# The first transform of a long convolution as 32-row by 64-column matrix blocks at four row positions of TensorE, two token tiles side by side

## The chip, the core and the metric

The kernel runs on one core of a Trainium2 chip. The core has TensorE (PE in the profile, with its weight loads as PEld), VectorE (DVE), ScalarE (ACT), GpSimd (POOL) and SyncE (SP). Each engine runs its own instructions in a fixed order and waits on semaphores for the others. Matrix results land in PSUM, from which ACT or DVE copy them to the on-chip memory. Transfers are issued by SP, POOL or ACT. The metric is the device time of one execution in microseconds; the kernel before takes 1782.84 us, the median of three runs (1781.9 to 1785.29).

## What is computed

There are 2048 tokens of 576 channels. A conditioning vector `c` gives six vectors of 576 numbers (shift, scale and gate for two halves). The first half is a layer norm, then a long convolution per channel by FFT with a kernel made from 128 complex poles per channel. The second half is a gated MLP that mixes over tokens.

```python
mod = (_silu(c) @ w_mod).reshape(c.shape[0], 6, 1, -1)
sa, ca, ga, sb, cb, gb = (mod[:, 0], mod[:, 1], mod[:, 2], mod[:, 3], mod[:, 4], mod[:, 5])
h = _layernorm(x, axis=-1) * (1 + ca) + sa
x = x + ga * _A_ref(h, A_re, A_im, B_re, B_im, C_re, C_im, log_dt, Dskip)   # y = irfft(rfft(h) * rfft(K))
h = _layernorm(x, axis=-1) * (1 + cb) + sb
x = x + gb * _B_ref(h, w_in, w_sp, b_sp, w_out)                             # gated MLP over tokens
```

Only the transform of `h` (with `ga` already multiplied in) is changed here.

## The kernel before

The work has two parts. The first, `ssm`, makes the convolution and takes roughly the first 420 us; the rest is the MLP, in which TensorE is busy nearly all the time. Inside `ssm` an FFT of 2048 tokens is taken as 32 by 64: a first transform over 32 tokens that lie apart, then a second over 64.

**The loop.** `for tick in range(NG + 4)` runs over 36 groups of poles. In each tick, for group numbers shifted by some ticks, `t_unit` (L428, phases), `s_unit` (L440, sine and cosine on ACT), `p_unit` (L445, products on DVE), `kg_unit` (L461, matmuls that make the convolution kernel) and `k1_unit` (L477, its own first transform) run; `e_unit` (L416, exponentials) runs every third tick. In ticks 0 to 7 the first transform of the tokens runs too, two tiles of 128 tokens in each tick. From tick 9 on its place is taken by the second transforms (`u_unit`, `z_unit`, `v_unit`, `y_unit`).

**One token tile** (`ln_unit`, L393). A tile is 128 rows: four groups of 32 tokens, so its transform matrix is four 32 by 32 blocks on the diagonal of a 128 by 128 matrix, once for the real and once for the imaginary part. DVE makes `n = (x - mean) * cga` (L397) and scales the matrix rows by the inverse deviation, `rt` (L399). TensorE then makes two outputs (real, imaginary) of 128 by 576, in two halves of 288 columns. Each half is a bf16 matmul that adds the transformed shift (L405: `cs`, 96 rows, times `gsp`) and a float32 matmul `rt` times `n` (L406), into one PSUM tile of the ring `ps`, which has two buffers. ACT copies each finished `ps` to `st1o` (L407), and POOL stores a whole tile, 128 by 2 by 576, to `u1_d` in DRAM (L408); `st1o` has two buffers too. From tick 9 on `u_load` (L521) reads `u1_d` back with all 2 by 16 by 4 blocks on the partitions, and `u_unit` multiplies by `fwd`, whose rows are in that order.

**The shift.** The constant part of `h`, `sga = sa * ga`, is the same for all tokens, so only the column sums of the transform matrix are needed. To keep float32 accuracy in bf16, `sga` is split into three bf16 parts and the sums too; the six useful products stand in six rows among the 96 of `cs` and `gsp`. `mod_unit(0)` makes `gsp` with four ACT copies and two DVE subtractions (L339 to L344), on partition ranges that start at 0, 32 and 64.

**Loads.** `r1_load(i)` (L361) brings the matrices of one pair of tiles, 256 KB in float32 and 96 KB in bf16; `ln_load(i)` (L357) brings four tiles of tokens, 1152 KB, into the buffer of the four tiles before the last four. Both are on SP.

**What sets the order.** The units are written tick by tick, but a scheduler of the language sorts the instructions of each engine by its own estimates, so that the order on an engine isn't the order of the code. Instructions issued through `mlp.tied` keep the program's order and appear with line 140 in the profile, which is the line of that helper.

Of the kernel before, what the change touches and what calls it, by code (L numbers as in the profile page):

```python
# [9 lines left out]
F32 = mybir.dt.float32  # L10
# [21 lines left out]
def consts():  # L32
# [8 lines left out]
    for j in range(4):  # L41
        s = slice(32 * j, 32 * j + 32)
        r1[0, s, s] = np.cos(ang)
        r1[1, s, s] = -np.sin(ang)
    r1t = np.zeros((128, 16, 2, 128))
    st4 = np.zeros((128, 16, 2, 64))
    for t in range(16):
        for g in range(4):
            th = ang + 2 * np.pi * b4[4 * t + g] * (k1 + 0.25) / 2048
            s = slice(32 * g, 32 * g + 32)  # L50
            r1t[s, t, 0, s] = np.cos(th)
            r1t[s, t, 1, s] = -np.sin(th)
            hh, g2 = divmod(g, 2)
            o = slice(32 * g2, 32 * g2 + 32)
            st4[64 * g2:64 * g2 + 32, t, hh, o] = np.cos(th).T / 2048
            st4[64 * g2 + 32:64 * g2 + 64, t, hh, o] = -np.sin(th).T / 2048

    import ml_dtypes
    part = r1t.sum(0)
    cs = np.zeros((96, 16, 2, 128))  # L60
    for i in range(3):
        rows = part.astype(ml_dtypes.bfloat16).astype(np.float64)
        cs[i] = rows
        if i < 2:
            cs[32 + i] = rows
        if i < 1:
            cs[64 + i] = rows
        part = part - rows

    def forward(th):  # L70
# [7 lines left out]
    for h, sg in ((0, 1.0), (1, -1.0)):  # L78
# [19 lines left out]
    f = np.float32  # L98
    small = np.concatenate([np.eye(128), r1[0], r1[1], forward(th), st3a, st3b, ones], axis=1)
    return {"c_small": small.astype(f), "c_st": st2.astype(f), "c_r1t": r1t.astype(f), "c_st4": st4.astype(f),  # L100
            "c_sel": sel.astype(ml_dtypes.bfloat16), "c_cs": cs.astype(ml_dtypes.bfloat16)}

# [50 lines left out]
def ssm(tc, I, x1_d, consts_s, dram, mod_d, mlp):  # L153
# [5 lines left out]
    with ExitStack() as ctx:  # L159
# [156 lines left out]
        sga = ep.tile([128, D], F32, name="sga", bufs=1)  # L316
        gsp = ep.tile([96, D], BF, name="gsp", bufs=1)

        def mod_unit(k):
# [15 lines left out]
            elif k == 1:  # L335
                V.scalar_tensor_tensor(v3(cga), src, 1.0, v3(gar), op0=ALU.add, op1=ALU.mult)
            elif k == 0:
                V.tensor_tensor(v3(sga), src, v3(gar), op=ALU.mult)
                A.activation(gsp, sga[:96], AF.Copy)  # L339
                V.tensor_tensor(sga[:96], sga[:96], gsp, op=ALU.subtract)  # L340
                A.activation(gsp[32:64], sga[32:64], AF.Copy)
                A.activation(gsp[64:], sga[64:96], AF.Copy)
                V.tensor_tensor(sga[64:96], sga[64:96], gsp[64:], op=ALU.subtract)
                A.activation(gsp[64:], sga[64:96], AF.Copy)  # L344
            else:
                mrow = ep.tile([128, D], F32, name="gar", bufs=1)
                if k == 4:
                    A.activation(v3(mrow), src, AF.Identity, bias=one)
                else:
                    A.activation(v3(mrow), src, AF.Copy)  # L350
                G.dma_start(mod_d[k - 3:k - 2], mrow[0:1])
# [16 lines left out]
        def ln_stats(i):  # L368
# [3 lines left out]
            if i < 2:  # L372
                junk = ep.tile([128, 2, D], F32, name="st1o")
                ss = ep.tile([128, 4], F32, name="ss")
# [17 lines left out]

        def ln_unit(b):  # L393
            i, j = divmod(b, 4)
            nm, r = lns[i]
            n = x4s[i][:, j]
            V.scalar_tensor_tensor(n, n, nm[:, j:j + 1], cga, op0=ALU.add, op1=ALU.mult)  # L397
            rt = ep.tile([128, 2, 128], F32, name="rt")
            V.tensor_scalar(rt, r1t[b // 2][0][:, b % 2], r[:, j:j + 1], None, op0=ALU.mult)  # L399
            o = ep.tile([128, 2, D], F32, name="st1o")  # L400
            for ri in range(2):
                pm = ps2()
                for h in range(2):
                    c = slice(HC * h, HC * h + HC)
                    T.matmul(pm[:, h, :HC], r1t[b // 2][1][:, b % 2, ri], gsp[:, c], start=True, stop=False)  # L405
                    T.matmul(pm[:, h, :HC], rt[:, ri], n[:, c], start=False, stop=True)  # L406
                A.activation(v3(o[:, ri]), pm[:, :, :HC], AF.Copy)  # L407
            G.dma_start(u1_d[:, b].rearrange("r p d -> p r d"), o)  # L408

# [109 lines left out]
        def u_load(c, i):  # L519
            st[c, i] = u1 = part("u1", 5)  # L520
            S.dma_start(by(u1, c), u1_d.rearrange("r b (g k) d -> (r b g) k d", k=32)[:, kr(c, i), chan(c)])  # L521

# [106 lines left out]
        r1_load(0)  # L629
        ln_load(1)  # L630
        S.dma_start(dsk, I["dsk"])
        r1_load(1)
# [17 lines left out]
        for tick in range(NG + 4):  # L650
# [53 lines left out]
            if j < 8:  # L704
                if j in (2, 4):
                    ln_stats(j // 2 + 1)
                for b in (2 * j, 2 * j + 1):
                    ln_unit(b)
                if j < 6:
# [1437 lines left out]
```

## Time and profile before

| | |
|---|---|
| median of the runs | 1782.84 us |
| the profiled execution, its own time | 1788.13 us |
| its span in the profile | 1786.3 us |
| TensorE busy over the span | 94% |
| first transform, first matmul to last store issued | 54.1 to 159.3 us |
| its matmuls | 64 in bf16 (L405), 64 in float32 (L406, two records each, 128 in all) |

The page of the profile gives busy times for the whole span. The first transform lies in one stretch of some 105 us, so the views that count here are those of that stretch: busy time of each engine in pieces of 10 us, groups of instructions, and waits. `PEclk` is the clock that TensorE was granted, 1.00 for full speed. Line numbers such as L406 are those of the kernel before. A float32 matmul leaves two records of a weight load and two of a matmul.

### The profile page before, as it was taken

How to read it: one execution, taken by the hardware profiler on the slowest of the kernel's cores; microseconds unless marked ns; L12 is line 12 of the kernel's file. 1: busy time of each engine (PE TensorE's matmuls, PEld its weight loads, DVE VectorE, ACT ScalarE, POOL GpSimd, SP SyncE). 2: the span in 40 equal slices, each digit the busy share in tenths (PEclk: the TensorE clock that was granted, in tenths of full speed). 3: DMA queues.
4: the chain of work that ended last, by engine and by line, in shares of the span. 5: the costliest groups of instructions: out<-in, count | busy, mean ns of one | idle time of the engine just before them, and what ended most of it. 6: DMA issues, size and time to landing. Idle time of an engine off the chain costs nothing.

```text
span 1786.3 us, 35743 instructions
## 1 busy us (share of the span) xinstructions
PE 1686.7 (94%) x14830; PEld 1255.3 (70%) x14830; DVE 1266.6 (71%) x2331; ACT 854.4 (48%) x1129; POOL 227.0 (13%) x364
## 2 busy tenths in 40 slices
PE   3599899998899999999989999999999999999999
PEld 1355555565455445777878888888888888888887
DVE  6785999966998998688889677688344468344432
ACT  4778999954477666445434444234222224122210
POOL 2111223332122211000000000000111100111100
PEclk9789999998999999999999999999999999999999
DMA  9465646679688779777665886773766573556531
GB/s 268 145 198 179 196 120 167 176 204 304 206 260 266 249 228 264 284 248 250 240 209 164 282 299 233 269 253 118 250 225 226 203 231 100 193 195 215 194 111 40
DMA packets 182193, 377.80 MB, mean 212 GB/s; under 512 B 37680, under 2 KB 101552, under 8 KB 181264
## 3 DMA queue, kind: packets, MB, share of 16 engines
q1 hardware_dynamic: 140000, 177.29, 33.1%
q0 software_dynamic: 36128, 171.57, 28.9%
q10 hardware_dynamic: 5904, 26.67, 3.7%
q8 instruction: 116, 1.90, 0.4%
q14 instruction: 45, 0.37, 0.1%
HBM read 264.73 MB, written 101.31 MB: 205 GB/s over the span
## 4 chain that ended last, share of the span: by engine, by line
PE 58%; DVE 10%; DMA 8%; issue 4%; ACT 1%; POOL 1%; SPq 0%; ACTq 0%; DVEq 0%; POOLq 0%
PE ps L140 54%; DMA zset<-set_d 2%; DMA wsst<-in_w_spT 1%; DVE zset L140 1%; DVE bsz L140 1%; DMA win_d<-wso 1%; DVE n L140 1%; DVE gt L140 1%; DVE rq L140 1%; PE pk L527 1%; ACT z L140 1%; PE pk L540 1%; DMA ue<-v_d 1%; DMA z_d<-z 1%; DVE wsp L140 1%
## 5 line engine op out<-in xcount | busy, mean ns | idle before, releaser
L140 PEld LDWEIGHTS <-zset 128*128 128x128 f16 x7182 | 702.8, 98 | 95.3 <-DVE zset L140 9.5
L140 PE MATMUL ps<-wsp,zset 128*128 128x256 f16 x6048 | 669.2, 273 | 9.1 <-DVE zset L140 7.5
L140 PE MATMUL pz<-wz,nt 128*128 128x512 f16 (+1 forms) x1120 | 222.5, 358 | 12.3 <-ACT nt L140 5.3
L140 ACT ACTIVATE z<-gt 128x1024 f16<-128x1024 f32 x56 | 59.0, 1054 | 285.4 <-DVE gt L140 285.4
L140 PEld LDWEIGHTS <-nt 128*128 128x128 f16 x1120 | 108.7, 98 | 119.9 <-ACT nt L140 6.9
L140 DVE SCALAR_TENSOR_TENSOR gt<-ps,sc,bsp 128x512 f32<-128x512 f32 x36 | 27.0, 750 | 206.0 <-PE ps L140 204.3
L140 PE MATMUL ps<-wout,z 128*128 128x288 f16 x1344 | 170.0, 286 | 0.0
L1855 POOL DMA_DIRECT2D zset<-set_d x96 | 50.9, 530 | 872.0 <-PE ps L140 626.1
L140 PEld LDWEIGHTS <-z 128*128 128x128 f16 x1344 | 131.5, 98 | 33.0
L140 DVE TENSOR_TENSOR raw<-raw 128x512 f32<-128x512 f32 (+2 forms) x228 | 119.1, 528 | 13.0 <-DMA raw<-z_d 8.7
L140 PE MATMUL ps<-n2o,zset 128*128 128x256 f16 x1134 | 128.2, 273 | 0.0
L140 DVE SCALAR_TENSOR_TENSOR gt<-ps,sc,gt 128x512 f32<-128x512 f32 (+1 forms) x180 | 122.2, 696 | 7.6
L140 ACT ACTIVATE zset<-raw 128x1792 f16<-128x1792 f32 x48 | 81.2, 1691 | 60.8 <-PE ps L140 27.0
L140 DVE TENSOR_TENSOR zset<-raw,zset 128x1792 f16<-128x1792 f32 x48 | 97.0, 2020 | 15.6 <-ACT zset L140 15.6
L140 DVE TENSOR_TENSOR z<-ps,z 128x512 f32<-128x512 f32 (+1 forms) x126 | 72.0, 599 | 36.8 <-ACT z L140 26.7
L140 ACT ACTIVATE wsp<-raw,sc 128x1792 f16<-128x1792 f32 x25 | 44.6, 1784 | 42.7 <-DVE raw L140 35.0
L140 ACT ACTIVATE z<-z,sc 128x1024 f32<-128x1024 f32 x21 | 24.1, 1148 | 75.6 <-DVE z L140 71.9
L435 DVE SCALAR_TENSOR_TENSOR ft<-ft,ps 128x1024 f32<-128x1024 f32 x36 | 43.8, 1217 | 18.0 <-ACT ft L434 18.0
L140 ACT ACTIVATE z<-z,nm,r 128x1152 f32<-128x1152 f32 x24 | 31.4, 1341 | 51.6 <-DVE nm L140 29.5
L140 ACT ACTIVATE z<-pz,sc 128x512 f32<-128x512 f32 (+1 forms) x96 | 51.6, 583 | 9.2 <-PE pz L140 4.6
L140 PE MATMUL ps<-n2q,wf 128*128 128x512 f16 x252 | 55.7, 379 | 0.0
L140 PE MATMUL ps<-wout,z1b 128*128 128x288 f16 x384 | 52.4, 286 | 0.0
(361 smaller groups left out, 2512.0 us busy)
## 6 DMA issues: line engine op xcount, KB each, us to landing
zset<-set_d POOLq DMA_DIRECT2D x96, 896.0 KB, 5.0
raw<-z_d SPq DMA_DIRECT2D x48, 512.0 KB, 5.6
set_d<-zset ACTq DMA_DIRECT2D x24, 896.0 KB, 6.1
z_d<-z POOLq DMA_DIRECT2D x32, 576.0 KB, 9.4
zset<-wa_d POOLq DMA_DIRECT2D x18, 896.0 KB, 4.9
raw<-in_w_spT SPq DMA_DIRECT2D x25, 512.0 KB, 4.5
set_d<-zset SPq DMA_DIRECT2D x12, 896.0 KB, 5.2
u_d<-st1o POOLq DMA_DIRECT2D x16, 576.0 KB, 3.8
```

The source lines that it names most:

```text
L140: return self.tc.keep_in_program_order(f(*a, **k))
L435: V.scalar_tensor_tensor(f, f, MAGIC, pa, op0=ALU.subtract, op1=ALU.subtract)
L527: T.matmul(pm, fwd, u1, start=True, stop=True)
L540: T.matmul(pm[:, w * j:w * j + w], cst[k // 8][:, k % 8], k1t[c][:, k, :w], start=True, stop=True)
L1855: self.nc.gpsimd.dma_start(o, self.set_d[f, j - 1] if j else self.wa_d[f])
```

## The change

The matrix blocks on the diagonal are no longer put into one 128 by 128 matrix with zeros elsewhere. Each 32-row group `g` of a tile is multiplied by its own 32 by 64 block (32 real and 32 imaginary outputs), with the group's rows as the row position in the array. Tile `t` of a pair writes output partitions `64 t` to `64 t + 63`, and group `g` writes its own bank: `pms[g // 2]`, half `g % 2`. A pair of tiles is done in two halves of 288 channels, each with 8 bf16 and 8 float32 matmuls, four copies of 128 by 576 in all (L415 of the new file) and two stores of 128 by 4 by 288.

The shift is now added for each row group, so `gsp` needs its six rows in every group of 32 partitions. The subtractions are made on all 128 partitions with a mask `msk`, a new small constant whose entries are 0 or -1 (from partition 3 on the first part is taken off, from 5 on the second). The constants `r1t` and `cs` shrink to 32 columns, 64 KB and 32 KB per pair; `cs` has 128 rows. `u1_d` becomes `[4, 16, 2, 32, D]`, and the rows of `fwd` are put in that order, so `u_load` reads as many pieces of the same size as before. `rt` has four buffers in place of two. `junk` in `ln_stats` takes the new shape of `st1o`, of the same size.

```diff
-    r1t = np.zeros((128, 16, 2, 128))
+    r1t = np.zeros((128, 16, 2, 32))
...
-            r1t[s, t, 0, s] = np.cos(th)
-            r1t[s, t, 1, s] = -np.sin(th)
+            r1t[s, t, 0] = np.cos(th)
+            r1t[s, t, 1] = -np.sin(th)
...
-    part = r1t.sum(0)
-    cs = np.zeros((96, 16, 2, 128))
+    part = np.stack([r1t[32 * g:32 * g + 32].sum(0) for g in range(4)])
+    cs = np.zeros((128, 16, 2, 32))
...
+        for r in ((0, 3, 5), (1, 4), (2,))[i]:
+            cs[r::32] = rows
         part = part - rows
+    msk = np.zeros((128, 2))
+    for g in range(0, 128, 32):
+        msk[g + 3:g + 6, 0] = -1.0
+        msk[g + 5, 1] = -1.0
...
-        u1_d = dram.tile([2, 16, 128, D], F32, name="u1_d")
+        u1_d = dram.tile([4, 16, 2, 32, D], F32, name="u1_d")
...
-                A.activation(gsp, sga[:96], AF.Copy)
-                V.tensor_tensor(sga[:96], sga[:96], gsp, op=ALU.subtract)
-                A.activation(gsp[32:64], sga[32:64], AF.Copy)
-                A.activation(gsp[64:], sga[64:96], AF.Copy)
-                V.tensor_tensor(sga[64:96], sga[64:96], gsp[64:], op=ALU.subtract)
-                A.activation(gsp[64:], sga[64:96], AF.Copy)
+                for i in range(2):
+                    A.activation(gsp, sga, AF.Copy)
+                    V.scalar_tensor_tensor(sga, gsp, msk[:, i:i + 1], sga, op0=ALU.mult, op1=ALU.add)
+                A.activation(gsp, sga, AF.Copy)
...
-            r1t[i] = ep.tile([128, 2, 2, 128], F32, name="r1t"), ep.tile([96, 2, 2, 128], BF, name="cs")
+            r1t[i] = ep.tile([128, 2, 2, 32], F32, name="r1t"), ep.tile([128, 2, 2, 32], BF, name="cs")
...
-        def ln_unit(b):
+        def ln_rows(b):
...
-            rt = ep.tile([128, 2, 128], F32, name="rt")
-            V.tensor_scalar(rt, r1t[b // 2][0][:, b % 2], r[:, j:j + 1], None, op0=ALU.mult)
-            o = ep.tile([128, 2, D], F32, name="st1o")
-            for ri in range(2):
-                pm = ps2()
-                for h in range(2):
-                    c = slice(HC * h, HC * h + HC)
-                    T.matmul(pm[:, h, :HC], r1t[b // 2][1][:, b % 2, ri], gsp[:, c], start=True, stop=False)
-                    T.matmul(pm[:, h, :HC], rt[:, ri], n[:, c], start=False, stop=True)
-                A.activation(v3(o[:, ri]), pm[:, :, :HC], AF.Copy)
-            G.dma_start(u1_d[:, b].rearrange("r p d -> p r d"), o)
+            rt = ep.tile([128, 64], F32, name="rt", bufs=4)
+            V.tensor_scalar(rt, r1t[b // 2][0][:, b % 2].rearrange("p r k -> p (r k)"), r[:, j:j + 1], None, op0=ALU.mult)
+            return n, rt, r1t[b // 2][1][:, b % 2].rearrange("p r k -> p (r k)")
+
+        def ln_pair(b):
+            pair = [ln_rows(b), ln_rows(b + 1)]
+            for h in range(2):
+                c = slice(HC * h, HC * h + HC)
+                o = ep.tile([128, 4, HC], F32, name="st1o")
+                pms = [ps2(), ps2()]
+                for t, (n, rt, cs) in enumerate(pair):
+                    for x, y, st in ((cs, gsp, True), (rt, n, False)):
+                        for g in range(4):
+                            rows = slice(32 * g, 32 * g + 32)
+                            T.matmul(pms[g // 2][64 * t:64 * t + 64, g % 2, :HC], x[rows], y[rows, c], start=st, stop=not st, skip_group_check=True)
+                for k, pm in enumerate(pms):
+                    A.activation(o[:, 2 * k:2 * k + 2], pm[:, :, :HC], AF.Copy)
+                G.dma_start(u1_d[:, b:b + 2, :, :, c].rearrange("g b r k d -> (b r k) g d"), o)
...
+        S.dma_start(msk, I["c_msk"])
```

Besides what the code says, the scheduler puts some instructions in another order, in ticks 0 to 9 and hardly behind them. Three places follow. The numbers behind a name tell one buffer from another; new line numbers are up to 8 higher than the old ones.

On PE, the start of the first pair of tiles in tick 0 before (`ps` is the PSUM ring, `gsp` and `cs` the shift, `ln_x` the tokens `n`, `rt` the scaled matrix):

```order
L405 LDWEIGHTS cs_144
L405 MATMUL ps_462<-gsp_105,cs_144 128x288
L406 MATMUL ps_462<-ln_x_119,rt_459 128x288
...
L405 MATMUL ps_468<-gsp_105,cs_144 128x288
L406 MATMUL ps_468<-ln_x_119,rt_459 128x288
...
L405 MATMUL ps_479<-gsp_105,cs_144 128x288
L406 MATMUL ps_479<-ln_x_119,rt_476 128x288
```

The same place in the changed kernel:

```order
L413 LDWEIGHTS cs_145
L413 MATMUL ps_466<-gsp_105,cs_145 64x288
...
L413 MATMUL ps_466<-ln_x_120,rt_460 64x288 x2
...
L413 MATMUL ps_466<-ln_x_120,rt_463 64x288 x2
...
L413 MATMUL ps_467<-ln_x_120,rt_460 64x288 x2
...
L413 MATMUL ps_467<-ln_x_120,rt_463 64x288 x2
```

Before, one `ps` takes two bf16 and two float32 matmuls of one tile. Now one `ps` takes two row groups of the first tile (two bf16, then two float32, the row that ends in x2) and the same two row groups of the second tile; the other two row groups go to the next `ps`.

On DVE in tick 2, around the statistics of the third block of tokens (`bs`, `mv`), before:

```order
L276 TENSOR_TENSOR t_ph_359<-t_ph_359,t_rnd_301 128x432
L387 BN_STATS bs_606<-ln_x_572 128x6 x3
L388 BN_AGGR mv_607<-bs_606 128x2
L387 BN_STATS bs_606<-ln_x_572 128x6 x2
...
L454 TENSOR_TENSOR pg_674<-et_405,ft_502 128x512
```

and now:

```order
L278 TENSOR_TENSOR t_ph_360<-t_ph_360,t_rnd_303 128x432
L462 TENSOR_TENSOR pg_723<-et_406,ft_519 128x512
L463 TENSOR_TENSOR pg_723<-et_406,ft_519 128x1024
L210 TENSOR_TENSOR t_sq0_629<-t_ph_360,pt_628 128x432
L388 BN_STATS bs_639<-ln_x_605 128x6 x3
```

The statistics stood ahead of the products `pg` of `p_unit` and now stand behind two of them.

On ACT ahead of tick 0, between two exponentials `et`, before:

```order
L341 ACTIVATE gsp_105<-sga_104 32x576
L342 ACTIVATE gsp_105<-sga_104 32x576
L376 ACTIVATE st1o_370,nm_368<-ln_x_147 128x576
L426 ACTIVATE et_405<-pk_410 128x512
L344 ACTIVATE gsp_105<-sga_104 32x576
```

and now:

```order
L343 ACTIVATE gsp_105<-sga_104 128x576
L377 ACTIVATE st1o_371,nm_369<-ln_x_148 128x576
L431 ACTIVATE et_406<-ps_407 128x1024
L345 ACTIVATE gsp_105<-sga_104 128x576
...
L434 ACTIVATE et_406<-pk_411 128x512
L431 ACTIVATE et_414<-ps_415 128x1024
```

One of the four copies to `gsp` is gone, and one of the four sums over a token tile (`nm`) moved ahead of the third exponential, where it stood behind it.

More of the change, by code (lines that the diff above doesn't have):

```diff
@@ L98, in consts @@
     f = np.float32
[L99 removed]
+    fwd = forward(th).reshape(2, 16, 4, 128).transpose(2, 1, 0, 3).reshape(128, 128)
+    small = np.concatenate([np.eye(128), r1[0], r1[1], fwd, st3a, st3b, ones], axis=1)
     return {"c_small": small.astype(f), "c_st": st2.astype(f), "c_r1t": r1t.astype(f), "c_st4": st4.astype(f),
[L101 removed]
+            "c_sel": sel.astype(ml_dtypes.bfloat16), "c_cs": cs.astype(ml_dtypes.bfloat16), "c_msk": msk.astype(f)}
 def bc(ap, shape):
@@ L316, in ssm @@
         sga = ep.tile([128, D], F32, name="sga", bufs=1)
-        gsp = ep.tile([96, D], BF, name="gsp", bufs=1)
+        gsp = ep.tile([128, D], BF, name="gsp", bufs=1)
+        msk = cp.tile([128, 2], F32, name="msk")
         def mod_unit(k):
@@ L372, in ln_stats @@
             if i < 2:
-                junk = ep.tile([128, 2, D], F32, name="st1o")
+                junk = ep.tile([128, 4, HC], F32, name="st1o").rearrange("p (a b) d -> p a (b d)", a=2)
                 ss = ep.tile([128, 4], F32, name="ss")
```

10 lines of the change are left out of this document (2 added, 8 removed).

## The prediction

> **What bounds the kernel now.** I read the busy times in pieces of 10 us over the first transform, then the groups of instructions there with what ended their waits, then single stretches of the timeline. The sum is made against the profiled execution:
>
> ```profile
> span 1786.3 us, 35743 instructions
> ```
>
> Its own time is 1788.13 us, 1.8 beyond its span and 5.3 above the median of 1782.84; I work out a difference and take it from the median.
>
> ```profile
> core 0: us, PE busy (x) PEld busy (x) DVE busy (x) ACT busy (x) POOL busy (x), PEclk, DMA share, GB/s
> 50.00:60.00 10.00, 3.85 (x10) 2.20 (x10) 8.69 (x13) 9.87 (x18) 0.00 (x0) 0.50 0.01 4
> 60.00:70.00 10.00, 5.53 (x18) 2.96 (x17) 8.20 (x25) 9.94 (x17) 0.73 (x1) 0.84 0.19 69
> 70.00:80.00 10.00, 8.98 (x35) 5.10 (x35) 9.64 (x20) 7.13 (x12) 6.00 (x8) 0.66 0.53 159
> 80.00:90.00 10.00, 5.46 (x72) 3.14 (x71) 5.01 (x12) 4.59 (x5) 0.73 (x1) 0.85 0.79 266
> 90.00:100.00 10.00, 7.84 (x52) 3.87 (x50) 8.93 (x28) 9.47 (x13) 3.74 (x5) 0.67 0.48 162
> ...
> 120.00:130.00 10.00, 8.09 (x90) 4.89 (x88) 9.35 (x30) 4.75 (x8) 1.88 (x3) 1.00 1.00 334
> ...
> 105.00:160.00 55.00, 50.93 (x539) 31.05 (x535) 37.78 (x80) 42.22 (x58) 8.88 (x13) 1.00 0.59 192
> 200.00:250.00 50.00, 48.45 (x674) 27.83 (x674) 46.05 (x71) 47.92 (x63) 14.49 (x24) 1.00 0.38 111
> ```
>
> Three regimes show. Up to 100 us PE is not the bound: ACT is nearly full in three of the five pieces, PE works at a granted clock of 0.50 to 0.85, and 80 to 90 us is a stall in which transfers run and no engine is full. From 105 to 160 PE has the clock whole and is busy 50.93 of 55 us, ACT 42.22. Behind, in the loop, PE (48.45 of 50) and ACT (47.92) are both nearly full, so I take it that time won or lost before 160 us reaches the end undiminished.
>
> Who waits for the first transform between 48 and 162 us, and then ACT between 105 and 160:
>
> ```profile
> L406 PE MATMUL ps<-ln_x,rt 128*128 128x288 f32 x128 | 47.3, 465 | 0.0
> L407 ACT ACTIVATE st1o<-ps 128x576 f32<-128x576 f32 x32 | 20.4, 647 | 14.9 <-DMA u_d<-st1o 8.1 <-PE ps L406 5.8 <-ACT et L426 0.3
> L408 POOL DMA_DIRECT2D u_d<-st1o x16 | 11.7, 731 | 72.3 <-ACT st1o L407 72.3
> L399 DVE TENSOR_SCALAR rt<-r1t,r 128x256 f32<-128x256 f32 x14 | 4.9, 352 | 9.0 <-PE ps L406 8.9
> ```
>
> ```profile
> L407 ACT ACTIVATE st1o<-ps 128x576 f32<-128x576 f32 x20 | 12.8, 650 | 7.4 <-PE ps L406 4.1 <-DMA u_d<-st1o 2.7 <-ACT et L426 0.3
> L328 ACT ACTIVATE mpart<-ps 128x576 f32<-128x576 f32 x3 | 2.0, 651 | 2.5 <-PE ps L326 2.4
> L350 ACT ACTIVATE gar<-ps 128x576 f32<-128x576 f32 x2 | 1.3, 651 | 1.8 <-PE ps L331 1.8
> ```
>
> PE carries 47.3 us of float32 records here, yet ACT waited for them only 5.8, of which 4.1 after 105 us and so 1.7 before. The larger wait of the copies, 8.1, is for stores.
>
> **The change part by part.**
>
> *The matmuls.* At full clock one half of one output starts 0.61 us after the other:
>
> ```profile
> 109.23 0.29 PE L405 MATMUL ps<-gsp,cs 96*128 96x288 bf16 x1
> ...
> 109.36 0.65 PE L406 MATMUL ps<-ln_x,rt 128*128 128x288 f32 x2
> ...
> 109.84 0.29 PE L405 MATMUL ps<-gsp,cs 96*128 96x288 bf16 x1
> ```
>
> A pair of tiles has 8 of these, 4.9 us. Changed, it has 16 pairs of a bf16 and a float32 matmul with as many columns streamed; one behind another that is 9.8 us. No 32-row block runs before, so overlap between row positions must be bounded. The nearest rows use four column positions:
>
> ```profile
> 126.75 1.89 PE L326 MATMUL ps<-wm,ec 96*32 96x288 f32 x22
> ...
> 128.47 0.41 PE L326 MATMUL ps<-wm,ec 96*32 96x288 f32 x2
> ```
>
> These 24 records are 12 float32 matmuls in 2.13 us. In one row, at 0.61 less the 0.13 between the bf16 and the float32 start (109.23 and 109.36), 0.48 each, they would take 5.8: four positions gave 2.7 times. The bounds for a pair are therefore 9.8 (nothing overlaps), 4.9 (only the two column halves do), 2.45 (the four rows do, the two tiles come one after the other), and 1.2 (all eight). Blocks are issued over the four rows of one tile, then over those of the other, so I take 2.45; at the efficiency of L326 a row group of four would make it 3.6.
>
> *A ring that takes turns.* Before, each of the two `ps` buffers is filled alone, and its copy (0.65) runs beside the next. Now both buffers fill in step over the two tiles, so both copies come at the end of a half, and the next half starts behind both. Without other PE work between, a pair holds PE for 1.2 + 1.3 + 1.2 = 3.7 us plus two hand-overs, against 4.9. At 4.9 of matmul it would be 6.2, which is a loss. About half the pairs have other matmuls between their halves in the new order. ACT thus still waits about 1.2 at a half that stands alone.
>
> *Gain on PE's side.* Up to 105 us the 1.7 that ACT waits for L406 is at stake; with turns I take 1.0. From 105 on ACT waits 4.1 + 2.4 + 1.8 = 8.3 us for L406 and for two other products that stand behind them on PE; 5 pairs (20 copies) lose 5 x 2.45 = 12.3 us of PE, so all 8.3 could go. ACT's own 42.22 and the 2.7 for stores stay. With the turns I take half, 4.2. Ends of both together: 0 and 10.
>
> *The shift.*
>
> ```profile
> L140 DVE TENSOR_TENSOR sga<-sga,gsp x2: 750/752/754, 47.0 to 50.4; 96x576 f32<-96x576 f32 x1, 32x576 f32<-32x576 f32 x1
> L339 ACT ACTIVATE gsp<-sga x1: 670/670/670, 46.3 to 46.3; 96x576 bf16<-96x576 f32 x1
> L341 ACT ACTIVATE gsp<-sga x1: 682/682/682, 49.0 to 49.0; 32x576 bf16<-32x576 f32 x1
> ```
>
> Copies of 32 and of 96 partitions last alike, so 128 will too: four copies become three on an ACT that is busy 9.87 of 10, gain 0.7 (0 to 0.7). DVE's two steps get a scalar operand and stay near 0.75; they have the time of the copies.
>
> The mask is one more load on SP, issued behind the second load of tokens. The nearest row is another small load of that time, which took 15.4 us from 28.9, to 44.3:
>
> ```profile
> L631 SPq DMA_DIRECT2D dsk<-in_dsk x1: 346/346/346, 28.9 to 28.9; - x1
> ...
> DMA to landing us min/median/max: 15.4/15.4/15.4
> ```
>
> It is needed at 47.0 (the first subtraction), so I take 0; a load later than that would delay by its lateness.
>
> *`rt`, loads and stores.* `rt` falls from 256 columns to 64, between 0 and 0.35 us less per tile, and its 8.9 us of waiting for `ps` goes with four buffers. DVE has 37.78 of 55 us after 105; I take 0. The loads of `r1t` and `cs` fall from 352 to 96 KB a pair, two issues as before. Stores stay two per pair on POOL (0.73 each, and L408 waits 72 us for its data), in runs of half the length, with 1,152 bytes each. Nobody but the next pair's copies waits for them; I take 0, from -1 to 1 per stall. The stalls:
>
> ```profile
> 88.28 0.65 ACT L407 ACTIVATE st1o<-ps 128x576 f32<-128x576 f32 x1 [5.37 <-DMA u_d<-st1o]
> ...
> 88.41 1.18 DVE L387 BATCH_NORM_STATS2 bs<-ln_x 128x6 f32<-128x288 f32 x3 [3.95 <-DMA ln_x<-in_x]
> ...
> 88.98 0.40 PE L405 MATMUL ps<-gsp,cs 96*128 96x288 bf16 x1 [4.54 <-ACT st1o L407]
> ...
> 90.24 1.15 ACT L442 ACTIVATE ft<-ft,consts_s 128x1024 f32<-128x1024 f32 x1
> ...
> 93.20 0.67 DVE L454 TENSOR_TENSOR pg<-et,ft 128x512 f32<-128x512 f32 x1
> ...
> 94.43 1.17 DVE L455 TENSOR_TENSOR pg<-et,ft 128x1024 f32<-128x1024 f32 x1
> ```
>
> ACT and DVE both wait for DMA until 88.3. With 256 KB less ahead, at 266 and 334 GB/s (the rows 80:90 and 120:130), the stalls at 88 and near 125 could end 1.0 and 0.8 earlier. Not all of it need lie in front of the awaited transfer: half, 0.9.
>
> *DVE's order in tick 2.* The statistics that started at 88.41 now stand behind the two products that ran at 93.20 and 94.43, and those need the sine at 90.24, which is behind the stalled copies on ACT. At the earliest the sine ends at 91.39 and the products, 0.67 and 1.17, at 93.2: at worst the statistics, and the chain behind them (mean, `n`, the next matmuls), come 4.8 us later, at best the chain is not urgent and DVE only swaps work, 0. ACT, busy 9.47 of 10 in that piece, sets the pace more than DVE does, so I take a third, 1.5.
>
> `u1_d`, `fwd` and `junk` are only other layouts: the loads from `u1_d` have pieces of the same size, `fwd` is permuted on the host; 0.
>
> Sum: 1.0 + 4.2 + 0.7 + 0.9 - 1.5 = 5.3 us. Profiled, 1788.1 becomes 1782.8; of the median 1782.8 becomes **1777.5 us**.
>
> **A rule against it.** PE changes between forms of block all the time:
>
> ```profile
> 119.21 0.14 PEld L468 LDWEIGHTS pk<-et 128*32 128x32 f32 x4 [0.39 <-issue]
> ...
> 120.04 0.10 PEld L405 LDWEIGHTS <-cs 96*128 96x128 bf16 x1 [0.17 <-issue]
> ```
>
> From 128-column blocks to 32-column ones and back there is 0.39 and 0.17 us of idle weight load. The Trainium skill, "TensorEngine Tiling (Array Packing)", Key Properties, says that changing the tiling mode drains TensorE, and these rows agree as to the sign. By that rule, if each half of a pair that stands apart paid 0.39 more than now, 16 x 0.39 = 6.2 us would be added, some 3 of them on the path, and the gain would be 2. By the rows the old form pays such gaps already, and my sum takes none.
>
> **Rivals.**
>
> *Slower by the clock.* The rows up to 100 us show that a PE with gaps is granted 0.50 to 0.85, 0.70 on average; from 105 it has 1.00 because it is busy throughout. The change takes PE work away: between 105 and 160 there remain 50.9 - 24.5 = 26.4 plus 12.3 = 38.7 us at full clock, in short bursts with waits for ACT between. At a granted 0.70 that is 55.3, and with the turns (1.3 and hand-overs, 5 pairs, 8.5 us at most, half covered) about 59.5, 4.5 more than the 55 now: the other terms (0.7 + 0.9 - 1.5) change nothing, so about 1787. It decides from a mean clock below 0.76, where 38.7 / 0.76 + 4.2 = 55. Against it: from 200 us on, with PE at 97%, the clock is whole, and gaps of 1.3 us are shorter than PE's 4.54 at 88.98, behind which the granted clock is 0.67. The Trainium skill, "TensorE: Matmul & The Clock Gate", Part 1, says that the clock is halved after an idle window of some 3.4 us and full again after a busy one; by that rule gaps of 1.3 us would not do it, and this rival would fall; the wait of 4.54 with 0.67 behind it agrees, but no row shows gaps of 1.3 us alone.
>
> *Little changes.* The clock falls somewhat, or ACT and the transfers give the pace: then the 5.2 of the matmuls shrink to 1 to 2, and the time stays within 0.2%, 3.6 us, which is about what a measurement of this kernel can tell from no change; 1781.
>
> *No overlap of row positions.* If the four rows run one after another, a pair needs 4.9 and takes turns besides: 6.2 in place of 4.9, 1.3 or more for the half of the 8 pairs that have no cover, 5 us, about 1788. If columns don't overlap either, 4.9 x 8 = 39 us, of which some 20 would be exposed, 1803. For it speaks only that no row of the trace shows row positions; against it L326.
>
> *More.* All eight positions at once, ACT without gaps and stalls that start earlier: 1.7 + 8.3 + 0.7 + 1.8, about 12 us, 1771.
>
> **How the numbers follow.** Forecast, with its own range of 3.6 to 9 us of gain (1774 to 1779), 0.46; more, 0.06; little changes, 0.18; clock, 0.18; no row overlap, 0.08; serial, 0.04. So faster 0.52, same 0.18, slower 0.30. For 8 in 10 the range leaves out the serial case and the far ends: 1768 to 1791.
>
> **What the new profile would show.** The new matmul line in groups of four records that start within 0.05 us, and some 1.2 us from a half's first bf16 to its last float32: overlap right. Starts 0.5 apart: wrong. ACT's waits for the new line after 105 us at 2 to 5 us, and less for the two other products: the gain's place is right. Granted clock of 1.00 from 105 on: no clock rival; below 0.8, it decides. Pairs of copies with an idle PE of 1.3 us beside them: the turns. In tick 2 the place of the statistics behind the products and the time of the first `n` after it, against 88.41: the 1.5. The last store of the first transform some 5 us before the present one at 159.3. The mask landing before its first use. The forecast is wrong if the matmuls don't overlap, if the clock falls, or if the loop from 160 us on does not simply start earlier.

## The result: no change, and the profile after

The changed kernel takes 1784.6 us (median of 12 runs, 1780.48 to 1788.39), the kernel before 1784.76 (12 runs): ratio 1.0001, 95% interval 0.999 to 1.0013. Twice more, beside other kernels and on two different chips, the ratio was 1.0000 (0.9987 to 1.0013) and 0.9984 (0.997 to 0.9997). A gain of 5.3 us was forecast, 0.3%; two of the three show none of it, the third about half.

The profiled execution took 1783.95 us, near its median; the one shown of before lay 3.4 us above its own. So the 4.5 us between the two spans are mostly chance, and only what repeats in further profiles counts. Part of the chance lies behind the part that was changed. The last plain sine of the loop (L443 before, L451 now) starts at 373.3 and 370.9 us in two profiles of before and at 367.7, 370.8 and 374.5 in three of the changed kernel; from there to the end of the span it is 1412.9 and 1410.5 us, and 1414.2, 1412.8 and 1411.7. What follows the loop thus differs by some 3.6 us, not much less than the effect that is looked for.

```profile
span 1781.8 us, 36128 instructions
```

Busy time by stage, changed kernel (columns as in the prediction):

```profile
core 0: us, PE busy (x) PEld busy (x) DVE busy (x) ACT busy (x) POOL busy (x), PEclk, DMA share, GB/s
50.00:60.00 10.00, 3.84 (x38) 1.42 (x38) 9.23 (x14) 9.94 (x19) 0.00 (x0) 1.00 0.00 0
...
120.00:130.00 10.00, 9.34 (x123) 4.46 (x123) 9.86 (x30) 8.70 (x12) 0.90 (x2) 0.83 0.33 119
...
140.00:150.00 10.00, 7.12 (x98) 3.15 (x103) 5.57 (x8) 9.18 (x13) 1.51 (x2) 0.63 0.31 119
150.00:160.00 10.00, 7.15 (x76) 3.74 (x76) 5.87 (x9) 6.55 (x9) 3.09 (x5) 0.50 0.51 163
...
105.00:160.00 55.00, 43.40 (x621) 22.80 (x618) 34.52 (x74) 41.96 (x57) 10.27 (x15) 0.81 0.53 175
200.00:250.00 50.00, 48.73 (x688) 28.58 (x688) 46.05 (x72) 47.94 (x64) 12.82 (x21) 1.00 0.37 106
```

From 105 to 160 us PE is busy 43.4 us in place of 50.9, and that at a granted clock of 0.81 in place of 1.00. ACT is busy 42.0 as before (42.2): it idles 13.0 us of the 55 where it idled 12.8. The loop behind, from 200 us, is unchanged.

The groups of the transform, 48 to 162 us, then ACT's groups from 105 to 160:

```profile
L413 PE MATMUL ps<-ln_x,rt 32*64 32x288 f32 x256 | 25.9, 550 | 0.0
L415 ACT ACTIVATE st1o<-ps 128x576 f32<-128x576 f32 x32 | 19.6, 649 | 10.0 <-DMA u_d<-st1o 6.6 <-issue 2.1 <-ACT ft L451 0.7
L400 DVE TENSOR_SCALAR rt<-r1t,r 128x64 f32<-128x64 f32 x12 | 3.1, 287 | 0.1
```

```profile
L415 ACT ACTIVATE st1o<-ps 128x576 f32<-128x576 f32 x20 | 12.4, 655 | 7.0 <-DMA u_d<-st1o 4.0 <-issue 2.1 <-ACT ft L451 0.7
L450 ACT ACTIVATE ft<-ft,consts_s 128x1024 f32<-128x1024 f32 x5 | 5.7, 1147 | 2.0 <-DVE ft L445 2.0
L442 ACT ACTIVATE ft<-ps,consts_s 128x1024 f32<-128x1024 f32 x5 | 5.6, 1119 | 1.5 <-PE ps L441 1.4
...
L331 ACT ACTIVATE mpart<-ps 128x576 f32<-128x576 f32 x2 | 1.3, 652 | 2.1 <-PE ps L329 2.1
```

The 4.1 us that ACT waited for the transform's matmuls are gone, as forecast, and so is one of the other two waits on PE (1.8; the other is 2.1, was 2.4). In their place stand stores (4.0, was 2.7), "issue" 2.1 (time in which the profile shows nothing that ACT waited for), DVE 2.0 and the phase product L441 1.4. The waits changed their names, not their sum.

The matmuls themselves did what the prediction took. One half of a pair, at full clock:

```profile
104.82 0.49 PE L493 MATMUL pk<-small,kab 128*64 128x128 f32 x4
105.33 0.31 PE L413 MATMUL ps<-gsp,cs 32*64 32x288 bf16 x2
105.45 0.64 PE L413 MATMUL ps<-ln_x,rt 32*64 32x288 f32 x2
...
105.99 0.71 PE L413 MATMUL ps<-ln_x,rt 32*64 32x288 f32 x13
106.63 0.54 PE L493 MATMUL pk<-small,kab 128*64 128x128 f32 x5
```

From 105.33 until other work starts at 106.63 a half holds PE 1.3 us, 2.6 per pair, against 4.9 before: row positions overlap.

### The profile page after: what moved, and what is told of

Same layout as the page of the kernel before. It is cut to its first block, busy times and chain, and to the rows that moved or that the text cites. A ratio compares the mean times of both kernels' runs of the same rounds, so it can differ in the third digit from the quotient of the medians.

```text
span 1781.8 us, 36128 instructions
## 1 busy us (share of the span) xinstructions
PE 1675.0 (94%) x15022; PEld 1240.9 (70%) x15022; DVE 1265.7 (71%) x2331; ACT 854.3 (48%) x1130; POOL 227.1 (13%) x364
## 5 line engine op out<-in xcount | busy, mean ns | idle before, releaser
L142 DVE TENSOR_TENSOR raw<-raw 128x512 f32<-128x512 f32 (+2 forms) x228 | 119.2, 528 | 11.8 <-DMA raw<-z_d 7.5
L443 DVE SCALAR_TENSOR_TENSOR ft<-ft,ps 128x1024 f32<-128x1024 f32 x36 | 43.9, 1219 | 19.8 <-ACT ft L442 19.8
L142 PE MATMUL ps<-n2q,wf 128*128 128x512 f16 x252 | 55.7, 379 | 0.0
```

Source lines behind the costliest of these rows:

```text
L142: return self.tc.keep_in_program_order(f(*a, **k))
L443: V.scalar_tensor_tensor(f, f, MAGIC, pa, op0=ALU.subtract, op1=ALU.subtract)
```

## Where the lead is lost: the transfers around the second load of tokens

I compare the kernels by the plain sine on ACT (L443 before, L451 now), which runs once per tick. At the second one after 100 us the changed kernel is ahead, and at the third it mostly isn't: its three profiles (two of them from e5 and e12, below) have 113.3, 114.0 and 113.5, then 130.0, 133.3 and 133.8; the first profile of before has 117.9 and then 133.1, its second (e11) 116.6 and 131.0. Between the two stands the last load of tokens (`ln_x`), and about 1 us behind it POOL issues a store of results (`u_d`). The rows are the issues, then the statistics that wait for the load and ACT's copies that wait for the store, before:

```profile
113.09 0.78 SPq L359 DMA_DIRECT2D ln_x<-in_x  x1
...
114.05 0.73 POOL L408 DMA_DIRECT2D u_d<-st1o  x1 [1.69 <-ACT st1o L407]
...
115.08 1.28 SPq L312 DMA_DIRECT2D wm<-in_w_mod  x2
...
120.65 1.18 DVE L387 BATCH_NORM_STATS2 bs<-ln_x 128x6 f32<-128x288 f32 x3 [1.90 <-DMA ln_x<-in_x]
...
124.83 1.19 ACT L407 ACTIVATE st1o<-ps 128x576 f32<-128x576 f32 x2 [2.71 <-DMA u_d<-st1o]
...
125.53 0.37 PE L432 MATMUL ps<-sel,lc 48*128 48x512 bf16 x1 [1.65 <-ACT st1o L407]
```

and changed:

```profile
107.19 0.39 SPq L360 DMA_DIRECT2D ln_x<-in_x  x1
...
108.36 0.75 POOL L416 DMA_DIRECT2D u_d<-st1o  x1 [1.43 <-ACT st1o L415]
...
109.61 1.30 SPq L314 DMA_DIRECT2D wm<-in_w_mod  x2
...
116.48 1.18 DVE L388 BATCH_NORM_STATS2 bs<-ln_x 128x6 f32<-128x288 f32 x3 [4.94 <-DMA ln_x<-in_x]
...
119.96 1.19 ACT L415 ACTIVATE st1o<-ps 128x576 f32<-128x576 f32 x2 [3.98 <-DMA u_d<-st1o]
```

The load goes out 5.9 us earlier, and the statistics start only 4.2 us earlier: 9.3 us from issue to use against 7.6. DVE now waits 4.94 us for it, against 1.90. Against the second profile of before, issued at 111.73 and used at 118.60, it goes out 4.5 us earlier and is used 2.1 us earlier. In both kernels two weight loads (`wm`) are transferred beside it, so they alone don't explain the longer load; nor is it the new transform's alone, for with the old one it takes 8.9 us in e8. Why it takes longer is not shown.

The store, too, lands late: 11.5 us after its issue, against 10.7 and 9.9 in the two profiles of before. ACT needs the store's buffer for its next copies and waits 3.98 us for it, against 2.71 and 1.97. PE's next matmul, the phase product, waits for that copy: in the old kernel 1.65 us, since PE still had the old transform's work until 123.9, and now 3.53 us, because it has nothing left. Behind that wait its clock falls. The phase product, the next modulation product (24 records) and the sum behind it, in the first profile, then in the second (e5) and third (e12) of the same kernel:

```profile
120.66 0.37 PE L440 MATMUL ps<-sel,lc 48*128 48x512 bf16 x1 [3.53 <-ACT st1o L415]
121.97 3.82 PE L329 MATMUL ps<-wm,ec 96*32 96x288 f32 x24
127.18 1.24 PE L334 MATMUL ps<-mpart,small 128*128 128x288 f32 x4
```

```profile
121.35 0.58 PE L440 MATMUL ps<-sel,lc 48*128 48x512 bf16 x1 [3.58 <-ACT st1o L415]
...
123.56 4.06 PE L329 MATMUL ps<-wm,ec 96*32 96x288 f32 x24
130.16 1.67 PE L334 MATMUL ps<-mpart,small 128*128 128x288 f32 x4
```

```profile
121.67 0.37 PE L440 MATMUL ps<-sel,lc 48*128 48x512 bf16 x1 [4.36 <-ACT st1o L415]
123.51 4.05 PE L329 MATMUL ps<-wm,ec 96*32 96x288 f32 x24
130.12 2.29 PE L334 MATMUL ps<-mpart,small 128*128 128x288 f32 x4
```

PE waits 3.5 to 4.4 us. The product of 24 records behind that takes 3.8 to 4.1 us; in the prediction's rows of before it took 2.13 at full clock. In the first execution the clock came back soon, in the two others later (it is 0.50 from 122.2 to 125.6 us in the first, from 120.9 to 131.0 and from 122.2 to 132.4 in the others): the same instruction L334 starts at 127.2 in one and at 130.1 and 130.2 in the others, 3 us apart, though they were only 0.7 to 1.0 apart at the end of the wait. By the windows, 125 to 135 us:

```profile
125.00:135.00 10.00, 9.10 (x175) 4.84 (x172) 8.64 (x23) 8.02 (x12) 1.73 (x3) 0.97 0.15 55
```

```profile
125.00:135.00 10.00, 9.61 (x130) 5.11 (x123) 7.95 (x21) 7.03 (x10) 0.53 (x1) 0.70 0.05 16
```

```profile
125.00:135.00 10.00, 10.00 (x130) 5.24 (x123) 7.38 (x20) 6.39 (x9) 0.52 (x1) 0.63 0.07 27
```

Granted clock 0.97, 0.70 and 0.63 for one program (first, second, third profile). The Trainium skill, "TensorE: Matmul & The Clock Gate", Part 1, says that the clock halves after an idle window of some 3.4 us that runs free of the kernel; these rows agree: waits of that length or somewhat more, and a clock behind them that differs from one execution to the next.

## The experiments

Theories: *transfers* (the token loads hold the pace, and what PE saves becomes a wait for them), *clock* (a freed PE is granted less clock), *ACT* (the copies hold the pace), *turns* (the two buffers of `ps` fill in step).

**e1: half the columns, kernel before.**

```diff
-                    T.matmul(pm[:, h, :HC], rt[:, ri], n[:, c], start=False, stop=True)
+                    T.matmul(pm[:, h, :HC // 2], rt[:, ri], n[:, HC * h:HC * h + HC // 2], start=False, stop=True)
```

> The kernel before, but each float32 matmul of the first transform covers only 144 of its 288 columns (so half of h is left out of the result): 4.9 us of matmul per pair of tiles become about 3.0, 15 us less in all, and nothing else is changed, neither loads nor buffers nor copies. If the transforms' matmuls are on the path after 105 us (the sum of the prediction), it is 3 to 8 us faster than before, like the term of 4.2 us. If the transfers at the two stalls set the pace, the time taken off PE only lengthens the waits for the token loads: within 2 us of before. If the granted clock takes the gain back, also within 2 us, but with a granted clock clearly under 1.00 between 105 and 160 us and no longer wait for the loads.

Ratio to before 0.9985 (0.9972 to 0.9998), 2.7 us, between what was expected of PE and of the two others. The records of L406 fall from 47.3 to 29.9 us, and the clock from 105 to 160 is 0.94; the statistics wait 3.3 us for loads, no longer than before (5.9 and 3.4). In the one profile of this kernel the loop's last sine starts at 365.9 us, 5.0 to 7.5 earlier than in the two of before, and the rest takes 1415.5. By the time little of what PE saves arrives, by the loop as much as the prediction's term; the order of the instructions moved too. How much PE's load weighed in the old kernel is left open.

**e2: every matmul three times, changed kernel.**

```diff
-                    for x, y, st in ((cs, gsp, True), (rt, n, False)):
+                    for x, y, st in 3 * ((cs, gsp, True), (rt, n, False)):
```

> The changed kernel with every matmul of the first transform issued three times (the accumulation starts anew each time, so the result stays): about 0.8 us per half of a pair become about 2.4, 4.8 per pair, the load that PE had before, some 25 us more in all. If the clock took the gain back, PE now has its clock of 1.00 from 105 us on again and the time does not rise, or falls by up to 4 us. If PE's load matters by itself, it is 5 to 15 us slower, because the two buffers also take turns (1.3 us a half). If the transfers set the pace, most of it is hidden: 0 to 5 us slower.

Ratio 1.0154 (1.0137 to 1.0171), 28 us slower, more than any theory gave. Its test was not clean: the repeated matmuls of a half, 72 records, take 2.6 to 4.6 us from the first start to the last behind 115 us, not 2.4, so PE has 6.5 us and more per pair, above the old 4.9, and the scheduler moved much else. What it does show is that more clock (0.94 from 105 to 160) doesn't pay for more work.

**e3 and e4: four token buffers of two tiles, in both kernels.** Lines of the changed kernel; the other has the same.

```diff
-            x4s[i] = ep.tile([128, 4, D], F32, name="ln_x")
-            S.dma_start(x4s[i], I["x"][:, 4 * i:4 * i + 4])
+            x2s[i] = ep.tile([128, 2, D], F32, name="ln_x", bufs=4)
+            S.dma_start(x2s[i], I["x"][:, 2 * i:2 * i + 2])
...
-                if j in (1, 3):
-                    ln_load(j // 2 + 2)
+                if j < 4:
+                    ln_load(j + 4)
```

> The changed kernel with the tokens in four buffers of two tiles instead of two of four (same bytes, same memory): the third and fourth block are loaded in halves, each as soon as one pair of tiles is done, so the waits of the statistics for the token loads (5.5 us in all) should go. If the transfers set the pace, it is 3 to 8 us faster than before; if the clock or ACT's copies do, within 2 us of before.

> The same four token buffers of two tiles in the kernel before. If the transfers set the pace of the changed kernel alone, since its PE is no longer the bound, this one gains less than the changed one does with them: 0 to 3 us faster than before, and the difference between the two is then what the matrix blocks are worth without that wait, 3 to 5 us. If the token loads bound both kernels alike, both gain the same.

The changed kernel gets 0.9977 (0.9968 to 0.9987), the old one 0.9995 (0.9983 to 1.0007), on one chip: 1782.56 against 1785.62 us. With the loads in halves the matrix blocks are worth 3.1 us; with the loads as they were, nothing that can be told. The sines show the same: e3 is 3.0 us ahead of e4 at the second (117.3 and 120.3) and still 3.2 us at the third (130.2 and 133.4), so the lead isn't lost between them any more. The statistics wait 1.9 us for loads in e3, where the changed kernel has 5.5, and the granted clock is 1.00 from 115 to 135. That is what the theory of transfers asked for. The smaller loads also change the order of other instructions on PE, ACT and DVE in both kernels; that this has a part in it isn't ruled out.

**e5: the changed kernel again.**

> The changed kernel again, beside the next three and on the same chip. It should be within 0.2% of before. Its second profile tells what differs from one execution to the next: if the granted clock around 50 us is 0.50 here (it was 1.00 in the first profile), the first copy of a transform should come at about 58 us, as before, in place of 55.7, and the last store of the transform at about 157 to 158.

Ratio 1.0000 (0.9987 to 1.0013). The first copy of the transform didn't move with the clock: it came at 55.6 us with a granted clock of 0.50, at 55.7 with 1.00. The 2.3 us against before (58.0) are thus not the clock. The last store came at 158.4 in place of 155.1, and that difference arose between 114 and 133 us, as shown above.

**e6: one buffer after the other.**

```diff
+                for k, pm in enumerate(pms):
-                for t, (n, rt, cs) in enumerate(pair):
-                    for x, y, st in ((cs, gsp, True), (rt, n, False)):
-                        for g in range(4):
+                    for t, (n, rt, cs) in enumerate(pair):
+                        for x, y, st in ((cs, gsp, True), (rt, n, False)):
+                            for g in (2 * k, 2 * k + 1):
```

> The changed kernel with the matmuls in the order of the buffers: all of one buffer (two row groups, both tiles), then its copy, then the other buffer, so that no half waits for two copies. If the turns ate the gain (tripling the matmuls cost 28 us where they should have fitted into the old kernel's PE time), it is 3 to 8 us faster than the changed kernel. If ACT and the transfers set the pace at this load of PE, it is the same within 2 us. If the four row positions are what makes the matmuls short, two at a time are longer, 0.8 becomes about 1.2 us per half, and it is 0 to 3 us slower.

Ratio 1.0019 (1.0005 to 1.0034). Nothing was gained, so the turns cost nothing that shows. In the order on PE the changed kernel already fills one buffer with both tiles and then the other in 10 of its 16 halves (the rows quoted with the change are one of them: `ps_466`, then `ps_467`); in the other six the two fill in step, and e6 changes those. Why it is slightly slower than the changed kernel was not followed up; the order differs in other places too.

**e7: every second copy on DVE.**

```diff
-                    A.activation(o[:, 2 * k:2 * k + 2], pm[:, :, :HC], AF.Copy)
+                    if k:
+                        V.tensor_copy(o[:, 2 * k:2 * k + 2], pm[:, :, :HC])
+                    else:
+                        A.activation(o[:, 2 * k:2 * k + 2], pm[:, :, :HC], AF.Copy)
```

> The changed kernel with every second copy from PSUM done by DVE instead of ACT: 16 x 0.65 = 10 us off ACT, about as much onto DVE (busy 34.5 of 55 after 105 us, but nearly full around 90 to 100). If ACT sets the pace of the first 160 us, it is 4 to 9 us faster than the changed kernel. If the transfers do, within 2 us. If the copies now wait on DVE behind the products of the loop, it is 2 to 8 us slower.

Ratio 1.0034 (1.0021 to 1.0047), 6 us slower. Ten microseconds off ACT bring nothing, which speaks against ACT as the pace, though DVE's load rose as much. That is the third of the expected ranges. Both kinds of copy now wait for PE (groups from 48 to 162 us, columns as before):

```profile
L416 DVE COPY st1o<-ps 128x576 f32<-128x576 f32 x16 | 12.0, 753 | 5.2 <-PE ps L413 5.2
...
L418 ACT ACTIVATE st1o<-ps 128x576 f32<-128x576 f32 x16 | 10.4, 650 | 13.3 <-PE ps L413 8.9 <-DMA u_d<-st1o 3.2 <-ACT ft L454 0.7
```

PE in turn waits for the copies of both engines; where the 6 us begin was not followed further.

**e8: the shift alone, in the kernel before.**

```diff
-                A.activation(gsp, sga[:96], AF.Copy)
-                V.tensor_tensor(sga[:96], sga[:96], gsp, op=ALU.subtract)
-                A.activation(gsp[32:64], sga[32:64], AF.Copy)
...
+                for i in range(2):
+                    A.activation(gsp, sga[:96], AF.Copy)
+                    V.scalar_tensor_tensor(sga[:96], gsp, msk[:, i:i + 1], sga[:96], op0=ALU.mult, op1=ALU.add)
+                A.activation(gsp, sga[:96], AF.Copy)
```

> The kernel before with only the shift made the new way: three copies on ACT in place of four and two masked subtractions on all 96 partitions, the mask as one more load. The prediction's term: 0.7 us faster, which five rounds can hardly tell from none; if the copies were on the chain that starts the transform, its first copy comes 0.7 us earlier at the same granted clock.

The first copy comes at 56.0 us, 2.0 earlier than before, where 0.7 was taken: the shorter chain of copies also lets the transform's first matmuls go ahead. Yet the ratio is 1.0005 (0.999 to 1.002). A lead at 56 us doesn't reach the end: the second sine of the loop is 3.5 to 3.7 us ahead of the two profiles of before (74.7 against 78.2 and 78.4), the third, behind the first load of tokens within the transform, no longer clearly (93.1 against 91.4 and 93.5).

**e9: a third buffer for the copied results, on top of e3.** The order on every engine is that of e3.

```diff
-                o = ep.tile([128, 4, HC], F32, name="st1o")
+                o = ep.tile([128, 4, HC], F32, name="st1o", bufs=3)
```

> The changed kernel with four token buffers of two tiles and a third buffer for the copied results (st1o); the order of the instructions on every engine is that of the kernel with the token buffers alone. In that one, ACT no longer waits for stores of the results after 105 us, and for 'issue' 2 us. If stores still hold the ring, 1 to 3 us faster than with the token buffers alone; if not, the same within 1.5 us.

Ratio 0.9959 (0.9944 to 0.9974) against e3's 0.9977. But the two were measured on different chips, and on this one the changed kernel itself has 0.9984 (e12), where it has 1.0000 on the other (e5). In the profiles the loop's last sine starts at 369.7 us, 1.5 later than in e3 (368.2), and the shorter time lies behind it, 1406.2 us against 1414.9. So it isn't shown that the third buffer gains anything.

**e10: five token buffers in place of e3's four.**

```diff
-            x2s[i] = ep.tile([128, 2, D], F32, name="ln_x", bufs=4)
+            x2s[i] = ep.tile([128, 2, D], F32, name="ln_x", bufs=5)
...
         r1_load(1)
+        ln_load(4)
...
-                if j < 4:
-                    ln_load(j + 4)
+                if j < 3:
+                    ln_load(j + 5)
```

> The changed kernel with five token buffers of two tiles, so that the fifth pair is loaded at the start and the others one tick earlier still. If PE's idle time at the token loads, and the lower clock behind it, is what eats the gain, another 1 to 3 us less than with four such buffers (0.23% faster than before there); if the rest is ACT, no more than 1 us.

Ratio 0.9941 (0.9925 to 0.9957): 1775.69 us, against 1787.43 of before and 1783.94 of the changed kernel on the same chip. It beats both, by more than was expected of it. The gain arises where the lead was lost: from the second to the third sine it takes 11.8 us (114.9 to 126.7), the changed kernel 16.7, 19.3 and 20.4. The last load of tokens now goes out at 87.7 us, and the store issued at 108.61 lands in 5.3 us, not 11.5. The statistics no longer wait, and PE keeps its clock where it fell (groups from 48 to 162 us, timeline, and windows of this kernel):

```profile
L388 DVE BATCH_NORM_STATS2 bs<-ln_x 128x6 f32<-128x288 f32 x16 | 6.5, 433 | 0.0
```

```profile
118.95 0.39 PE L440 MATMUL ps<-sel,lc 48*128 48x512 bf16 x1
119.81 1.89 PE L329 MATMUL ps<-wm,ec 96*32 96x288 f32 x22
121.53 0.41 PE L329 MATMUL ps<-wm,ec 96*32 96x288 f32 x2
```

```profile
115.00:125.00 10.00, 9.03 (x151) 4.94 (x147) 5.95 (x10) 9.43 (x14) 1.53 (x2) 1.00 0.55 176
125.00:135.00 10.00, 7.95 (x145) 4.48 (x138) 6.04 (x10) 8.92 (x13) 2.06 (x3) 1.00 0.47 154
...
105.00:160.00 55.00, 44.13 (x634) 22.82 (x628) 35.70 (x64) 45.52 (x61) 10.27 (x15) 0.84 0.53 174
```

No wait stands ahead of L440, and the modulation product takes 2.13 us again. The order is another one here too: two matmuls for the exponentials (L433) stand ahead of L440, which in the changed kernel come behind it. ACT is busy 45.5 of 55 us in place of 42.0, and the last store goes out at 151.8. The same five buffers were not tried in the kernel before: its matrices for a pair of tiles take 352 KB against 96, and the fifth buffer doesn't fit beside them. So the memory that the smaller matrices free is part of what the change is worth.

**e11 and e12: both kernels once more.**

> The kernel before once more, for a second profile: the first one was 3.3 us above the median of its runs. If the clock theory holds, PE's clock is again whole from 105 to 160 us, with PE busy 50 of 55, and the span is shorter only by what happens up to 60 us and in the later part: the last store of the transform comes at 157 to 159.

> The changed kernel a third time, for a third profile. By the clock theory, PE waits about 3.5 us before the phase product near 121 us in every execution, and the clock behind that wait is either near 0.8 (as in the first profile) or near 0.5 (second); the 24 records of the modulation product right behind it then take 2.5 or about 4 us, and all behind them, the last store included, is 3 us earlier or later by that.

Before: 0.9996 (0.9983 to 1.0009), last store at 157.2 us, granted clock 1.00 from 105 to 160 again:

```profile
105.00:160.00 55.00, 51.68 (x603) 31.84 (x600) 38.40 (x81) 42.55 (x58) 10.47 (x16) 1.00 0.59 196
```

Changed: last stores at 155.1, 158.4 and 159.0 us in three profiles, before at 159.3 and 157.2. The wait and the slow product were there each time. The two values expected for that product were wrong: it takes 3.8 to 4.1 us always, and what differs is how long the low clock lasts.

## Why the prediction was wrong

The forecast was 1777.5 us, faster at 0.52; it is unchanged, which had 0.18. The time lies in the range.

- **The matmuls: right.** 2.45 us per pair were taken, 2.6 measured. 9.8 and 4.9 fall.
- **The ring that takes turns: wrong, and in part a misread order.** The code fills both buffers in step; the order on PE, quoted with the change, fills them one by one in 10 of the 16 halves. The cost of 1.3 us a half doesn't show, and e6 found nothing to regain. It had only lowered the gain, so it isn't why the forecast was too fast.
- **Gain on PE's side, 1.0 + 4.2: this step failed.** Up to 105 us the gain is there: the first sine behind 100 us starts at 101.6, 102.2 and 101.7 in the changed kernel, at 106.2 and 104.9 before. From 105 us on, ACT's waits on PE did go, from 8.3 us to 2.1 + 1.4 as far as the rows show. I took the time as won because ACT's busy time and its wait for stores "stay". But a wait that ends earlier lets the next one begin: ACT idles 13.0 us where it idled 12.8, and its wait for stores didn't stay, it rose from 2.7 to 4.0. What came to be late next were the transfers around the second load of tokens: the load, for which DVE waits 4.94 us, and the store beside it, for which ACT, and through it PE, waits. I had read the stall near 125 us only as a place where smaller loads would help, and did not ask what its issue time and its 7.6 us would do to a kernel that reaches it 4 us earlier. Stores were taken at 0.
- **The shift, 0.7: too small at its place, and worth nothing at the end.** The first copy is 2.0 us earlier (e8), the time the same.
- **Loads, 0.9: wrong.** The second load takes 9.3 us from issue to use, in place of 7.6 and 6.9 in the two profiles of before, despite 256 KB less; the cause stays open. The first, issued at 75.94 and used at 84.23, takes 8.3 us; 9.4 in the first profile of before and 7.6 in the second, so nothing can be told.
- **DVE's order in tick 2, 1.5: wrong, nothing.** I took the products to be behind the stalled copies. In the new order the sine ran at 72.1 us and the products at 80.3 to 82.2, before the load had landed; the statistics waited 0.6 us for the load, not for the products.
- **The rival of the clock: the mechanism was right, its price too high.** The mean from 105 to 160 is 0.81, 0.78 and 0.78, just above the 0.76 from which it was to decide. I had argued that gaps would be 1.3 us, too short; one of 3.5 to 4.4 arose, out of the wait for the store.
- **"Little changes"** came true, and both causes that it named show in the traces: the transfers give the pace, and the clock falls. What each costs isn't told apart. It stood beside the forecast with 0.18, so it was seen, but not held for likely.

How the lost lead divides among the wait for the load, the wait for the store and the clock behind it is not settled by an experiment: a kernel that fills PE's wait with other matmuls wasn't run, because the scheduler then orders everything behind it anew, and every kernel here that changes a load changes the order too. The traces show that the part of the clock varies by 3 us from one execution to the next.

## What to carry to other kernels

When an engine is relieved, follow the lead to the next transfers that others wait for, and ask when they are issued and how long they then take: here a load that went out 4.5 to 5.9 us earlier was used 2.1 to 4.2 us earlier. A relieved TensorE also has less work to cover such a wait; here it waited 3.5 to 4.4 us in place of 0.9 to 1.7, and its clock from 105 to 160 us was 0.78 to 0.81 in place of 1.00. Look then at what the change frees: here the memory of the smaller matrices, spent on one more token buffer, brought 0.6% against before, where the shorter matmuls alone brought between nothing and 0.16%.

## What was not expected of the hardware

The four matmuls of a kind in a `ps`, 32 by 64 blocks in two row positions and two column positions, ran with starts some 3 to 20 ns apart, so a `ps` of 4 bf16 and 4 float32 matmuls needs about 0.4 us from its first to its last start. The clock also fell where no long wait stands. In the changed kernel from 139 to 146 us:

```profile
141.51 0.33 PE L413 MATMUL ps<-gsp,cs 32*64 32x288 bf16 x4 [0.22 <-ACT st1o L415]
141.63 0.69 PE L413 MATMUL ps<-ln_x,rt 32*64 32x288 f32 x8
144.51 0.47 PE L413 MATMUL ps<-gsp,cs 32*64 32x288 bf16 x4 [2.19 <-ACT st1o L415]
144.70 1.24 PE L413 MATMUL ps<-ln_x,rt 32*64 32x288 f32 x8
```

The longest gap is 2.19 us, and the same group of eight records takes 1.24 us behind it against 0.69 ahead. The granted clock is 1.00 from 139.3 to 142.7 us, with PE busy 2.2 of these 3.4 us and no gap above 0.6, and 0.50 from 142.7 on: here a PE with short work between waits was slowed like one that stands still. By the rule of the Trainium skill cited above, a window idle for 3.4 us, the clock would have stayed here; the rows differ from it in this.
